# Two layers of windowed attention and MLP on one core: the bias of the second MLP matrix kept in SBUF, and another order for the row maxima of a layer's first unit

## The chip, the cores and the metric

The kernel runs on one core of one Trainium2 chip. The time is device microseconds from a timed run of the whole program; three runs of the kernel before gave 1558.01, 1560.52 and 1563.2 us, so the median is 1560.52 us. The engines are named as the profile names them: PE is TensorE's matmul, PEld its weight load, DVE is VectorE, ACT is ScalarE, POOL is GpSimd, SP is SyncE, which here issues most DMAs.

## The reference

The input is one sequence of 2048 rows by 640 columns. Two layers run one after the other with the same weights; each is an attention block and an MLP block with a residual:

```python
x = A_x
for _ in range(2):
    x = x + A(layernorm(x), wqkv, wo)
    x = x + B(layernorm(x), w1, b1, w2, b2)
# A: 32 heads of 20; query i sees keys i-255..i; softmax; @ wo
# B: h = y @ w1 + b1;  h = max(h, 0)**2;  out = h @ w2 + b2
```

## The kernel before

**Units.** The rows are cut into 8 groups of 256. A group in a layer is a unit, so there are 16 units, u = 0 to 15; u = 0 and u = 8 are the first units of the layers. A unit's attention is worked in 8 quads of 4 heads each. Dense products are done three times over in two-byte floats (high times high, high times low, low times high), so TensorE has many short matmuls (`mm3`, L339).

**One unit's stages.** `stage_qk` and `stage_v` make q, k and v. For each quad, `max_quad` computes the scores once to take each row's maximum ("m" step), `exp_quad` computes them again with the maximum folded in and takes the exponential ("s" step, L825, with masks on POOL L854 and DVE L863), and `pv_quad` multiplies with v ("v" step, L931). `load_o` and `stage_o` divide and apply wo (L1056 adds to the residual), a layer norm follows (L365 to L378), `stage_y` or `y_cross` transposes y, and `stage_f` does the MLP: for each two of the 12 chunks of h, ACT takes the relu with b1 (L1120), POOL squares (L1124), ACT casts the high part (L1127), DVE subtracts for the low part (L1130). Then the second matrix follows and DVE adds to the residual (L1159).

**The bias of the second matrix.** Each `stage_f` first calls `add_b2`: SP loads b2, spread over 128 partitions, into one of the two rotating "xt" buffers (L1069), and POOL adds it to the residual in four pieces (L1076). The xt buffers also hold the rows that a layer norm loads (L430) and the y of `stage_o`. `ln_cross`, which loads the rows of a later unit, is put behind these additions in the plan.

**The row maxima.** A unit that is not the first of its layer has four quarters of keys per window (`quarters(u)` is true). Its scores lie in two PSUM tiles of three banks, `bb6[0]` and `bb6[1]`; each tile's maxima are one merge (L717) and one reduction (L720), and those of the second tile are put into the list `behind`. The function `tops()` issues what lies there; `pv_quad` calls it after its products are issued, and those products use a free half bank of `bb6[1]`. A layer's first unit has no earlier rows; its branch takes eight maxima per quad, each with the mask added (L683), alternating between the tiles (e = 0, 1) for each of four windows.

**What sets the order.** All instructions of all engines are put in order by hand. A planner in the kernel (`Job`, `post`, `pump`) keeps a clock for each engine with booked durations, issues jobs whose start lies within 250 ns of TensorE's planned time, and takes lower `prio` numbers first; a DMA books its size over a rate as traffic. `together` walks through the steps of a unit's quads, makes the maxima of quads that lie `LEAD` = 3 ahead within the v steps, and fills with dense work whenever a step isn't ready. Each engine runs its own queue in order. The maxima of unit 0 are made by `flow`, before the loop over the units; those of unit 8's quads 0 to 2 are made in unit 7's v steps, and its other five in its own.

The flag `later` is passed in `together` alone:

```python
max_quad(m, kind == "v" and quarters(what[1] // NQ))
```

**The start.** During the first units the weights are still loaded and split into high and low parts (`convert`, L271 on ACT, L272 on DVE); the second matrix comes in 12 loads issued by ACT (L324), and b1 is loaded by SP (L1369), behind the work of `load_o(0)`.

Of the kernel before, what the change touches and what calls it, by code (L numbers as in the profile page):

```python
# [10 lines left out]
F32 = mybir.dt.float32  # L11
# [3 lines left out]
ALU = mybir.AluOpType  # L15

P = 128
Q = P // 2
S = 2048
D = 640  # L20
# [4 lines left out]
T = 256  # L25
# [20 lines left out]
def kernel(ctx: ExitStack, tc: tile.TileContext, x, wqkv, wo, w1, b1, w2, b2, out):  # L46
    nc = tc.nc
# [3 lines left out]
    sb = ctx.enter_context(tc.tile_pool(name="sb", bufs=1))  # L51
# [14 lines left out]
    maskw = sb.tile([P, 2 * P], BF16, name="maskw")  # L66
# [15 lines left out]
    for h in range(2):  # L82
        nc.gpsimd.tensor_copy(drop[h * Q:(h + 1) * Q], edges[h * Q:(h + 1) * Q, :, h * Q:(h + 1) * Q])
    b1s = sb.tile([P, FC], F32, name="b1s")
    kts = []
    for i in range(3):
        kts.append(sb.tile([P, NP, T], F16, name=f"kt{i}"))
# [56 lines left out]
    def post(eng, cost, fn, *deps, wait=0.0, prio=1, **kw):  # L144

        j = Job(eng, cost, fn, [d for d in deps if d is not None], now[0] + wait, prio, **kw)
        k = len(pend)
        while k and pend[k - 1].prio > prio:
            k -= 1
        pend.insert(k, j)  # L150
        return j
# [5 lines left out]
    def dma(fn, size, *deps, n=1, cost=450.0, prio=1, **kw):  # L157

        return post("S", n * cost, fn, *deps, prio=prio, size=size, **kw)
# [18 lines left out]
    def need(*js):  # L178

        for j in js:  # L180
            while j.end is None:
                pass_time()
            now[0] = max(now[0], j.end)
# [453 lines left out]
    bbjobs = []  # L637
    bb6 = [ps.tile([P, 3, 512], F32, name=f"bb{e}") for e in range(2)]

    def banks():  # L640
        need(*bbjobs)
        bbjobs.clear()
        return bb6

    def quarters(u):

        return u % NG != 0

    def by_tiles(pieces):

        at, order = {}, []
        for k, (tile, cols, put) in enumerate(pieces):
            order.append((at.get(tile, 0), k, put))
            at[tile] = at.get(tile, 0) + cols
        for _, _, put in sorted(order, key=lambda o: o[:2]):
            for e in range(2):
                put(e)

    behind = []

    def tops():

        for f in behind:
            f()
        behind.clear()

    def max_quad(n, later=False):

        u, qd = divmod(n, NQ)
        g = u % NG  # L670
        qt, cur, prev = qts[u], kts[u % 3], kts[(u - 1) % 3]
        G = qd // GQ
        if (u, G) not in mxs:
            mxs[u, G] = sb.tile([P, 2, 2 * GQ, 2], F32, name="mx", bufs=2)
        mx = mxs[u, G]
        need(trips[u, 0, qd], trips[u, 1, qd])
        bb = banks()

        accum = {(e, w): mx[:, e, (2 * qd + w // 2) % (2 * GQ), w % 2:w % 2 + 1] for e in range(2) for w in range(4)}

        def reduce(e, w, v, mask, cols):
            bbjobs.append(post("D", 113 + 1.047 * cols, lambda:
                               nc.vector.tensor_tensor_reduce(out=v, in0=v, in1=mask, scale=1.0, scalar=-3.0e38,  # L683
                                                              op0=ALU.add, op1=ALU.max, accum_out=accum[e, w]),
                               prio=urgency["turn"]))

        if quarters(u):
            flat = [b.rearrange("p a n -> p (a n)") for b in bb]
            pieces = []
            for w in range(4):  # L690
                j, i = divmod(w, 2)
                p, at = 2 * qd + j, 5 * Q * w
                cuts = sorted({0, 5 * Q, *(z - at for z in (512, 1024) if 0 < z - at < 5 * Q)})
                for o0, o1 in zip(cuts, cuts[1:]):
                    for h in range(2):
                        for kt, lo, hi, to in ((prev, 0, T - i * P, i * P), (cur, T - i * P, 3 * P, i * P - T)):
                            a, b = max(lo, o0 + h * Q), min(hi, o1 + h * Q)
                            if a >= b:
                                continue

                            def put(e, kt=kt, a=a, b=b, to=to, h=h, p=p, i=i, o=at + a - h * Q):
                                r, rows = slice(64 * e, 64 * e + 3 * DH), slice(64 * h, 64 * (h + 1))
                                nc.tensor.matmul(flat[e][rows, o:o + b - a], qt[r, p, i * P + 64 * h:i * P + 64 * (h + 1)],  # L703
                                                 kt[r, p, a + to:b + to], start=True, stop=True,
                                                 tile_position=(64 * e, 64 * h))

                            pieces.append((h, b - a, put))
            by_tiles(pieces)
            now[0] += 690.0
            apart[0] = True  # L710
            for e in range(2):
                wins = flat[e][:, :4 * 5 * Q].rearrange("p (w c) -> p w c", c=5 * Q)
                later = maskq.bitcast(mybir.dt.uint16).unsqueeze(1).to_broadcast([P, 4, Q])
                most = mx[:, e, 2 * qd % (2 * GQ):2 * qd % (2 * GQ) + 2, :].rearrange("p n i -> p (n i)")

                def merge(wins=wins, later=later):
                    nc.vector.copy_predicated(wins[:, :, 4 * Q:], later, wins[:, :, :Q])  # L717

                def top(wins=wins, most=most):
                    nc.vector.tensor_reduce(most, wins[:, :, Q:], axis=mybir.AxisListType.X, op=ALU.max)  # L720

                def both(merge=merge, top=top):
                    j = post("D", 330, merge, prio=urgency["turn"])
                    bbjobs.append(post("D", 1130, top, j, prio=urgency["turn"]))
                    mxjobs[u, G] = list(bbjobs)

                behind.append(both)
                if not (later and e):
                    tops()
        else:  # L730
            for w in range(4):
                j, i = divmod(w, 2)
                for e in range(2):
                    r, p = slice(64 * e, 64 * e + 3 * DH), 2 * qd + j
                    nc.tensor.matmul(bb[e][:, w % 3, w // 3 * T:w // 3 * T + (1 + i) * P], qt[r, p, i * P:(i + 1) * P],
                                     cur[r, p, :(1 + i) * P], start=True, stop=True)
            now[0] += 530.0
            apart[0] = True
            for w in range(4):
                j, i = divmod(w, 2)  # L740
                for e in range(2):
                    to = bb[e][:, w % 3, w // 3 * T:w // 3 * T + (1 + i) * P]
                    if i:
                        reduce(e, w, to, maskw, 2 * P)
                    else:
                        reduce(e, w, to, maskw[:, P:], P)
            mxjobs[u, G] = list(bbjobs)

    mxjobs = {}

# [215 lines left out]
    ols = {}  # L966
# [98 lines left out]

    def add_b2(u):

        b2s = sb.tile([P, D], F32, name="xt", tag="xt", bufs=2)
        load = dma(lambda: nc.sync.dma_start(b2s, bass.AP(tensor=b2.tensor, offset=b2.offset, ap=[[0, P], [1, D]])),  # L1069
                   P * D * 4)  # L1070
        js = []
        for i in range(2):
            for h in range(2):
                hs = slice(h * HD, (h + 1) * HD)
                js.append(post("G", 827, lambda x1=x1s[u, i], hs=hs:
                               nc.gpsimd.tensor_tensor(x1[:, hs], x1[:, hs], b2s[:, hs], op=ALU.add), load, prio=2))  # L1076
        return js

    def y_cross(u):
# [22 lines left out]
    def stage_f(u, ahead=None):  # L1102
# [3 lines left out]
        need(*js)  # L1106
        y2 = y2s.pop(u)
        b2j = add_b2(u)
        hh = sb.tile([P, 2, FC, T], F16, name="hh", tag="hh", bufs=1)
        hj = []  # L1110
# [119 lines left out]
    def together(ns, ms, dense, cost, share=1.0, whole=True, after=None, pace=0):  # L1230
# [26 lines left out]
        for k, (part_, what, m) in enumerate(ts):  # L1257
# [17 lines left out]
            if m is not None:  # L1275
                max_quad(m, kind == "v" and quarters(what[1] // NQ))
# [90 lines left out]
    flow(todo, rest)  # L1367
    load_o(0)
    dma(lambda: nc.sync.dma_start(b1s, b1.rearrange("(c p) -> p c", p=P)), 8192, *ols[0][2], prio=2)  # L1369

    while not all(j.end is not None and j.end <= now[0] + LOOK for j in bbjobs):
        c = next(rest)
# [56 lines left out]
```

## Time and profile before

| What | Value |
|---|---|
| median of 3 runs | 1560.52 us (1558.01 to 1563.2) |
| profiled execution: its time, its span | 1561.46 us, 1559.6 us |
| mean granted TensorE clock | 0.997 |
| busy: PE, PEld, DVE, ACT, POOL | 98%, 77%, 67%, 43%, 29% |
| DMA moved | 162.16 MB, mean 104 GB/s |
| SP's DMA queue | 38.7% of 16 engines |

A share of busy time is an average over the whole span. The granted clock is 1 where TensorE runs at 2.4 GHz and 0.5 at 1.2 GHz. In rows of a timeline a bracket says how long the engine was idle before the instruction and what ended this.

### The profile page before, as it was taken

The page shows a single profiled execution, that of the slowest core. Times are in us where ns is not written, and L with a number is a line of the kernel's source. Part 1 is how long each engine was busy: PE and PEld are TensorE (multiplying, and loading weights), DVE is VectorE, ACT ScalarE, POOL GpSimd, SP SyncE. Part 2 cuts the span into 40 slices and gives each one's busy share as a digit, 9 for nine tenths or more (in the row PEclk, how much of TensorE's full clock was granted, in tenths as well). Part 3 has the DMA queues.
Part 4 walks back from the last instruction along what each step waited for, and adds up shares of the span by engine and source line. Part 5 has one row for each costly group of instructions (what it writes and reads, how often), then busy time and mean ns, then how long its engine had stood idle before and what let it go on. Part 6 is the DMA issues. An engine that isn't in the chain of part 4 may idle for free. (4 is left out here: it accounts for less than half of the span.)

```text
span 1559.6 us, 58897 instructions
## 1 busy us (share of the span) xinstructions
PE 1533.5 (98%) x25822; PEld 1198.6 (77%) x25822; DVE 1043.3 (67%) x2244; ACT 669.7 (43%) x1365; POOL 451.8 (29%) x847
## 2 busy tenths in 40 slices
PE   8998999999999999999999999999999999999999
PEld 6666778787787877878777787877878777786777
DVE  8878775666757667675666757667675676667642
ACT  4565435334453443435343453444435335354422
POOL 1223314232141331413224141321413214142412
PEclk9999999999999999999999999999999999999999
DMA  9975354352534424344462434425243342542120
GB/s 271 209 201 127 80 121 92 106 114 54 123 88 114 105 74 126 69 126 89 99 130 63 119 91 119 100 70 132 67 126 89 94 117 65 122 90 59 30 68 18
DMA packets 248745, 162.16 MB, mean 104 GB/s; under 512 B 96552, under 2 KB 232232, under 8 KB 248488
## 3 DMA queue, kind: packets, MB, share of 16 engines
q1 hardware_dynamic: 242120, 148.89, 38.7%
q10 hardware_dynamic: 6368, 9.50, 2.1%
q8 instruction: 202, 3.31, 0.9%
q14 instruction: 55, 0.45, 0.1%
HBM read 84.68 MB, written 52.95 MB: 88 GB/s over the span
## 5 line engine op out<-in xcount | busy, mean ns | idle before, releaser
L825 ACT ACTIVATE pt<-bb 128x640 f32<-128x640 f32 (+2 forms) x512 | 311.9, 684 | 167.6 <-PE bb L840 148.9
L854 POOL TENSOR_SCALAR_AFFINE_SELECT pt<-pt 64x256 f32<-64x256 f32 x448 | 199.3, 445 | 582.1 <-ACT pt L825 560.0
L339 PE MATMUL acc<-y,w_s 128*128 128x256 f16 x2880 | 330.2, 274 | 1.2 <-DVE y L390 1.2
L339 PE MATMUL acc<-w_s,hh 128*128 128x320 f16 (+1 forms) x2340 | 326.7, 297 | 0.1
L339 PEld LDWEIGHTS <-w_s 128*128 128x128 f16 x2880 | 276.4, 98 | 40.9 <-issue 2.0
L339 PEld LDWEIGHTS <-hh 128*128 128x128 f16 x2340 | 222.1, 98 | 86.8 <-issue 0.4
L720 DVE TENSOR_REDUCE mx<-bb 128x4 f32<-128x1024 f32 x224 | 273.2, 1224 | 6.8
L339 PE MATMUL acc<-yT,wq_s 128*128 128x256 f16 x2250 | 259.1, 273 | 3.0 <-DVE qd L537 1.2
L339 PEld LDWEIGHTS <-wq_s 128*128 128x128 f16 x2400 | 229.6, 98 | 37.3 <-issue 4.3
L863 DVE COPY_PREDICATED_SCALAR pt<-drop,zero 128x256 f32 x224 | 99.9, 497 | 134.3 <-ACT pt L825 133.8
L1130 DVE TENSOR_TENSOR hh<-r,hh 128x256 f16<-128x256 f32 x192 | 98.3, 525 | 110.8 <-ACT hh L1127 105.7
L931 PE MATMUL pv<-pt,vt 64*32 64x192 f32 (+5 forms) x3840 | 166.7, 302 | 0.9 <-DVE y L390 0.6
L943 ACT COPY ot<-pv 128x256 f32<-128x256 f32 x128 | 47.6, 372 | 276.1 <-PE bb L931 247.2
L1124 POOL TENSOR_TENSOR r<-r 128x256 f32<-128x256 f32 x192 | 121.9, 655 | 127.9 <-ACT r L1120 125.3
L931 PE MATMUL bb<-pt,vt 64*32 64x128 f32 (+3 forms) x3584 | 153.5, 301 | 0.0
L717 DVE COPY_PREDICATED bb<-maskq,bb 128x256 f32<-128x256 uint16 x224 | 93.8, 423 | 85.7 <-PE bb L703 80.0
L931 PEld LDWEIGHTS pv<-pt,vt 64*32 64x32 f32 (+1 forms) x3840 | 125.5, 106 | 31.7 <-issue 3.7
L339 PE MATMUL acc<-wo_s,od 128*128 128x320 f16 x960 | 139.6, 299 | 2.2 <-ACT od L1024 2.0
L339 PE MATMUL acc<-wq_s,yT 128*128 128x320 f16 x900 | 132.1, 302 | 5.0 <-DVE qd L537 4.2
L1120 ACT ACTIVATE r<-acc,b1s 128x256 f32<-128x256 f32 x192 | 81.1, 476 | 98.6 <-PE acc L339 96.5
L339 PEld LDWEIGHTS <-od 128*128 128x128 f16 x960 | 90.9, 98 | 40.6 <-ACT od L1024 2.3
L339 PEld LDWEIGHTS <-yT 128*128 128x128 f16 x900 | 87.1, 98 | 40.0 <-issue 6.2
(103 smaller groups left out, 1476.3 us busy)
## 6 DMA issues: line engine op xcount, KB each, us to landing
qt<-qk SPq DMA_DIRECT2D x30, 480.0 KB
kt<-qk SPq DMA_DIRECT2D x30, 480.0 KB
o<-ot SPq DMA_DIRECT2D x256, 42.0 KB
qk<-qd SPq DMA_DIRECT2D x15, 640.0 KB
od<-o SPq DMA_DIRECT2D x14, 640.0 KB
qk<-yl SPq DMA_DIRECT2D x13, 640.0 KB
xt<-in_A_x_dram SPq DMA_DIRECT2D x16, 320.0 KB
x<-in_A_x_dram SPq DMA_DIRECT2D x16, 320.0 KB
```

Source lines behind the costliest of these rows:

```text
L339: nc.tensor.matmul(acc, lhs(a, c), rhs(b, c), start=(k == 0), stop=(k == 3 * nk - 1))
L717: nc.vector.copy_predicated(wins[:, :, 4 * Q:], later, wins[:, :, :Q])
L720: nc.vector.tensor_reduce(most, wins[:, :, Q:], axis=mybir.AxisListType.X, op=ALU.max)
L825: return lambda: nc.scalar.activation(room_of(box)[:, a:b], bank[:, a:b], AF.Exp, scale=SCALE / (QS * QS))
L854: nc.gpsimd.affine_select(out=m, in_=m, pattern=[[0, 4], [-1 if k else 1, Q]], base=0, fill=0.0, compare_op=ALU.is_gt if k else ALU.is_ge, ...
L863: nc.vector.copy_predicated(m, drop[:, k:k + 1, :].bitcast(mybir.dt.uint16).to_broadcast([P, 4, Q]), zero.unsqueeze(1).to_broadcast([P, 4, ...
L931: nc.tensor.matmul(pv[h][32 * jj:32 * (jj + 1), q0 * Q:(q0 + w) * Q], vf[r, c:c + 32], boxes[e]["pt"][r, a:b], start=(k == 0), stop=(k == ...
L943: nc.scalar.copy(ot[:, qd % 2], to)
L1120: nc.scalar.activation(box["r"], acc[:, f, :], AF.Relu, bias=b1s[:, f0 + f:f0 + f + 1], scale=1.0 / (YS * WS))
L1124: nc.gpsimd.tensor_tensor(box["r"], box["r"], box["r"], op=ALU.mult)
L1130: nc.vector.tensor_sub(hh[:, 1, f, :], box["r"], hh[:, 0, f, :])
```

## The change

b2 gets a tile of its own, loaded once, behind b1's load; `add_b2` uses it in all 16 units. In the branch for a layer's first unit the maxima are issued tile by tile; those of the second tile go through `behind`, and `tops()` is called at once where `later` isn't set.

```diff
+    b2s = sb.tile([P, D], F32, name="b2s")
...
-            for w in range(4):
-                j, i = divmod(w, 2)
-                for e in range(2):
-                    to = bb[e][:, w % 3, w // 3 * T:w // 3 * T + (1 + i) * P]
-                    if i:
-                        reduce(e, w, to, maskw, 2 * P)
-                    else:
-                        reduce(e, w, to, maskw[:, P:], P)
-            mxjobs[u, G] = list(bbjobs)
+            def each(e):
+                for w in range(4):
+                    i = w % 2
+                    reduce(e, w, bb[e][:, w % 3, w // 3 * T:w // 3 * T + (1 + i) * P], maskw[:, (1 - i) * P:], (1 + i) * P)
+                mxjobs[u, G] = list(bbjobs)
+
+            each(0)
+            behind.append(lambda: each(1))
+            if not later:
+                tops()
...
     def add_b2(u):
-        b2s = sb.tile([P, D], F32, name="xt", tag="xt", bufs=2)
-        load = dma(lambda: nc.sync.dma_start(b2s, bass.AP(tensor=b2.tensor, offset=b2.offset, ap=[[0, P], [1, D]])),
-                   P * D * 4)
         js = []
         for i in range(2):
             for h in range(2):
                 hs = slice(h * HD, (h + 1) * HD)
                 js.append(post("G", 827, lambda x1=x1s[u, i], hs=hs:
-                               nc.gpsimd.tensor_tensor(x1[:, hs], x1[:, hs], b2s[:, hs], op=ALU.add), load, prio=2))
+                               nc.gpsimd.tensor_tensor(x1[:, hs], x1[:, hs], b2s[:, hs], op=ALU.add), *b2load, prio=2))
         return js
...
     dma(lambda: nc.sync.dma_start(b1s, b1.rearrange("(c p) -> p c", p=P)), 8192, *ols[0][2], prio=2)
+    b2load = [dma(lambda: nc.sync.dma_start(b2s, bass.AP(tensor=b2.tensor, offset=b2.offset, ap=[[0, P], [1, D]])),
+                  P * D * 4, *ols[0][2], prio=2)]
```

## Rows read from the trace of the kernel before

**Rows 1.** Engine shares of the page: busy us, share of the span, instructions.

```profile
PE 1533.5 (98%) x25822; PEld 1198.6 (77%) x25822; DVE 1043.3 (67%) x2244; ACT 669.7 (43%) x1365; POOL 451.8 (29%) x847
```

**Rows 2.** Busy time by stretches: length, busy of each engine, PEclk, DMA share, GB/s.

```profile
0.00:160.00 160.00, 145.16 (x1837) 109.77 (x1838) 128.84 (x344) 83.36 (x164) 40.75 (x82) 0.97 0.75 198
160.00:725.00 565.00, 562.93 (x10215) 443.22 (x10213) 383.46 (x755) 239.19 (x482) 161.92 (x305) 1.00 0.42 101
...
830.00:1320.00 490.00, 489.38 (x8696) 384.70 (x8694) 329.51 (x647) 208.59 (x426) 145.15 (x271) 1.00 0.39 98
1320.00:1510.00 190.00, 184.76 (x3359) 141.69 (x3358) 124.79 (x248) 80.59 (x163) 55.15 (x105) 1.00 0.29 74
```

**Rows 3.** Waits of PE from 160 to 1320: us in total, times, longest.

```profile
PE bb L840 <- issue: 2.3, 3, 1.1
```

**Rows 4.** DMA issues of the bias: count, KB of each.

```profile
xt<-in_B_b_dram SPq DMA_DIRECT2D x16, 320.0 KB
```

**Rows 5.** Timeline of SP near 719: start, us, instruction.

```profile
719.45 0.44 SPq L1069 DMA_DIRECT2D xt<-in_B_b_dram  x1
```

**Rows 6.** Timeline of POOL: start, us, instruction, count, idle before and its releaser.

```profile
723.03 0.86 POOL L1076 TENSOR_TENSOR x<-x,xt 128x320 f32<-128x320 f32 x1 [6.62 <-DMA xt<-in_B_b_dram]
...
247.39 0.86 POOL L1076 TENSOR_TENSOR x<-x,xt 128x320 f32<-128x320 f32 x1 [8.83 <-DMA xt<-in_B_b_dram]
...
253.59 2.09 POOL L1076 TENSOR_TENSOR x<-x,xt 128x320 f32<-128x320 f32 x2
```

**Rows 7.** Timeline of DVE, the low parts of h near 253 and 258.

```profile
253.53 1.43 DVE L1130 TENSOR_TENSOR hh<-r,hh 128x256 f16<-128x256 f32 x2 [1.92 <-ACT hh L1127]
...
258.69 0.75 DVE L1130 TENSOR_TENSOR hh<-r,hh 128x256 f16<-128x256 f32 x2
```

**Rows 8.** Timeline of PE near 258.

```profile
258.54 0.75 PE L840 MATMUL bb<-qt,kt 62*64 62x128 f16 x37 [0.33 <-DVE ot L946]
```

**Rows 9.** Timeline of SP from 129 to 145.

```profile
131.24 0.40 SPq L1369 DMA_DIRECT2D b1s<-in_B_b_dram  x1
136.49 0.36 SPq L1069 DMA_DIRECT2D xt<-in_B_b_dram  x1
```

**Rows 10.** Timeline of ACT from 122 to 142, loads and conversions of w2.

```profile
122.97 0.33 ACTq L324 DMA_DIRECT2D kt<-in_B_w_dram  x1
...
128.22 0.74 ACT L271 ACTIVATE w_s<-kt 128x640 f16<-128x640 f32 x1 [1.77 <-DMA kt<-in_B_w_dram]
...
131.81 0.34 ACTq L324 DMA_DIRECT2D kt<-in_B_w_dram  x1
...
138.81 1.36 ACT L271 ACTIVATE w_s<-kt 128x640 f16<-128x640 f32 x2
141.15 0.80 ACT L389 CAST y<-tr 128x384 f16<-128x384 f32 x2 [0.98 <-PE tr L403]
```

**Rows 11.** Busy time by stretches, as rows 2, around 139.

```profile
128.00:139.60 11.60, 8.37 (x178) 5.92 (x176) 11.05 (x25) 5.76 (x11) 3.04 (x6) 1.00 0.53 149
139.60:146.40 6.80, 5.80 (x58) 4.28 (x59) 5.77 (x11) 4.50 (x8) 1.51 (x1) 0.53 0.02 5
```

**Rows 12.** Timeline of DVE, maxima of unit 8's first quad.

```profile
743.95 0.30 DVE L683 CUSTOM_DVE_ANT_0 bb<-bb,maskw 128x128 f32<-128x128 f32 x1 [1.03 <-PE bb L931]
...
746.20 0.14 DVE L683 DVE_READ_ACCUMULATOR2_ANT mx<- 128x1 f32 x1
```

**Rows 13.** Waits of DVE from 725 to 830: us in total, times, longest.

```profile
DVE bb L683 <- PE bb L931: 2.0, 2, 1.0
```

**Rows 14.** Timeline of PE near 140.

```profile
140.24 1.30 PE L403 MATMUL tr<-ident,xt 128*128 128x128 f32 x5 [1.78 <-DVE xt L378]
```

**Rows 15.** Timeline of DVE near 139.

```profile
138.34 1.22 DVE L720 TENSOR_REDUCE mx<-bb 128x4 f32<-128x1024 f32 x1
139.49 0.60 DVE L378 TENSOR_SCALAR xt<-x,bmv 128x640 f32<-128x640 f32 x1
```

**Rows 16.** Timeline of PE near 1441.

```profile
1441.23 0.45 PE L339 MATMUL acc<-wo_s,od 128*128 128x320 f16 x2 [1.97 <-ACT od L1024]
```

## The prediction

> **What bounds the kernel now.** I read the engine shares first: TensorE is busy for 1533.5 of 1559.6 us, 98%, and no other engine passes 67% [rows 1]. An average can hide stages, so the busy time by stretches comes next [rows 2]. From 160 to 725 us TensorE is busy for 562.93 of 565.00 us, from 830 to 1320 us for 489.38 of 490.00. What is not busy lies at the two ends: 160.00 - 145.16 = 14.8 us in the first 160 us and 190.00 - 184.76 = 5.2 us from 1320 to 1510. Then TensorE's own waits from 160 to 1320 us: the largest group is 2.3 us "issue" [rows 3], and the next, 0.3 us, is one wait that comes up below. Over 1160 us, some 13 of the 16 units, nothing that another engine or a DMA does late reaches TensorE, apart from these. An edit can shorten the time only by taking TensorE work away (this one takes none) or at the ends; it can lengthen it by making something late that is now covered.
>
> **The first edit, the bias.** Before, each of the 16 calls of the second dense stage loads 320 KB [rows 4] into one of the two "xt" buffers, and four GpSimd additions wait for it. After, one load lands in a tile of its own, and 15 go: 15 x 0.328 = 4.9 of 162 MB. In steady units the load issues at 719.45 and the first addition starts at 723.03, 3.6 us later [rows 5, 6]. GpSimd stands still before it, 6.62 us there and 8.83 us in another unit at 247.39 [rows 6], because the addition is first in its queue. But what queues behind it (the squares L1124 and the masks L854) is made well ahead of TensorE: none of TensorE's waits in the middle is for GpSimd. So:
> - Taken off SyncE: 15 issues of 0.44 us [rows 5]. What stands behind them on that queue starts sooner by as much; nothing on TensorE waits for it. 0 us.
> - The additions: the same 64 (four a unit), the same 0.86 us [rows 6]. They start when the stage opens, in the gap in which GpSimd now waits. Four take 3.5 us, the gaps are 6.62 and 8.83 us. They then no longer lie between the squares, where they slow VectorE: at 253.53 two L1130 take 1.43 us beside the two additions of 253.59, at 258.69 a pair without them 0.75 us [rows 6, 7]. I let 1.43 - 0.75 = 0.68 us come off the chain L1130, L717, L720, L717, L720, L946 there, at whose end TensorE waits 0.33 us at 258.54 [rows 8]. That wait goes: -0.3 us. It is the only TensorE wait in the middle that I can tie to the bias. Bounds: 0 if the squares alone keep L1130 slow, -0.33 if not; nearest row says -0.3.
> - The Trainium skill, "SBUF — State Buffer", section "Who interferes with whom", says that a VectorE instruction with two SBUF inputs and a GpSimd instruction that reads SBUF shut each other out for a whole instruction. The 1.43 us agree. By that rule the squares shut L1130 out as well, so moving the additions alone might give 0 here instead of -0.3 us.
> - The buffers: "xt" rotates over four allocations per unit where it was five. The next layer norm's loads take the slots of the two y tiles, read long before. No wait appears; none of TensorE's waits in the middle is on that path. 0 us.
> - The single load is put behind b1's, which SyncE issues at 131.24, so it goes out at about 131.7 where the first bias load now goes at 136.49 [rows 9]. Nothing on SyncE stands between. It is 5 us earlier, in a stretch where three loads of the second MLP matrix start (the first at 131.81) [rows 10]. The DMA engines are 0.53 busy at 149 GB/s there [rows 11], so full rate by these rows is about 281 GB/s (an estimate) and 0.328 MB cost 1.17 us. A load issued at 122.97 was awaited until 128.22, 5.25 us later; one issued at 131.81, held up by 1.17 us, lands at 138.2, and its conversion on ScalarE starts at 138.81 now [rows 10]. Cover of 0.6 us there, and of 0.98 us more before TensorE is touched, since ScalarE's next step on the way to it, L389 at 141.15, has that much idle time in front of it [rows 10]. So 0; the price when it fails is the slower rival below. The planner, which books 1.0 us of traffic (size over rate) at this point, may shift those conversions by as much.
>
> **The second edit, the row maxima.** The branch for a layer's first unit issues its eight maxima tile by tile instead of alternating, in both layers; total work is the same. "Behind the products" needs the flag that is set only when the maxima of this unit are made inside the v turns of a unit with four quarters: with a lead of three quads these are the second layer's first three quads, 24 of the 128 maxima. For the other 13 quads only the order changes: 0 us. At the first of the three, the second maximum, which is on the second tile, waits 1.03 us until the products with v end, and the six behind it are held [rows 12]. VectorE has two such waits from 725 to 830 us, 2.0 us in all [rows 13]. With the first tile's four in front they are filled. So VectorE gains 2.0 us at most, where TensorE does not wait for it: its waits over this stretch are among those of the middle [rows 3]. On the path: 0 us. Bounds: below, nothing, since no wait is there to shorten; above, the four late maxima could hold the next quad's scores in each of three quads: seven take 746.34 - 743.95 = 2.39 us [rows 12], four so 1.4, three times that 4.1 us. I take 0, the value of the waits that are in the rows now, and because the planner puts dense matmuls ahead of whatever waits.
>
> **The sum.** -0.3 + 0 + 0 = -0.3 us. The profiled execution took 1561.46 us (span 1559.6), 0.94 above the median of 1560.52. So 1561.2 against the profiled execution, 1560.2 against the median.
>
> **Rivals.**
> - *Faster: the start falls into another order.* The order of instructions is worked out by a greedy planner, so each edit may shuffle what follows it. From 128 to 139.6 us TensorE is idle for 11.60 - 8.37 = 3.2 us, from there to 146.4 for 1.0 us [rows 11], 4.2 us together; the longest wait, 1.78 us [rows 14], is for VectorE's L378, which starts at 139.49 because a reduction of 1.22 us, L720, stands ahead of it [rows 15]. After these waits the granted clock is 0.53 from 139.6 to 146.4 [rows 11], so most of it is at 1.2 GHz, where 5.80 us are busy: 5.80 x 0.47 = 2.7 us lost. All of it gone: -6.9 us, 1553.6; more likely the 1.78 us and the clock, -4.5 us, 1556. For it: the edit moves a DMA right there. Against it: nothing in the edit moves L717/L720 or L378 on purpose.
> - The Trainium skill, "TensorE: Matmul & The Clock Gate", section "HAM oscillation — how this bites in real kernels", says that waits of the engine bring its clock down and the work behind starts slow. Here the row after 139.6 agrees, but a wait of 1.97 us at 1441 is followed by no slow row (clock 1.00 for 1320 to 1510) [rows 2, 16]. By the rule alone every such gap would be worth more than its length; by the rows only the cluster at the start is.
> - *Slower: the one bias load collides with the second matrix's loads.* If it delays them by more than 0.6 us, ScalarE, which takes its queue in order, stands at the conversion of 138.81; from 0.6 + 0.98 = 1.6 us on, the transposed second half of y behind it (L389), which TensorE needs next, is late, and there it decides. One delay of 1.17 us is under that; if each of the three loads loses as much, the last comes 3.5 us late: 3.5 - 1.6 = 1.9 us of TensorE wait, and another stretch at 1.2 GHz like the one seen, 2.7 us: +4.6 us, 1565.1. For it: 0.75 of the DMA share is in use over the first 160 us [rows 2]. Against it: at that very point 0.53 [rows 11].
> - *The maxima held behind the products make the next scores late*: +4.1 us, 1564.6. Against it: the whole stretch has no such wait to begin with.
> - *The flag does nothing* (three quads only, no wait on TensorE): this is inside the forecast; the time would be the same.
>
> **How the numbers follow.** Forecast, no change that can be told: 0.69. Other order at the start: 0.18, of which about 0.14 pass 4.7 us. Load collision 0.08, late maxima 0.05. A difference under 0.3% (4.7 us) is what a measurement of this kernel can hardly tell from none: the three runs alone lie from 1558.01 to 1563.2. Small reorderings at the two ends, which hold 14.8 + 5.2 us of waits, carry 0.05 of the forecast out on either side. So faster is 0.14 + 0.05 = 0.19; slower 0.05 and, since both slower rivals end close to the bound, about half of their 0.13, together 0.12; same the rest, 0.69. The range reaches 1.7 us past the partial faster rival and to the two slower ones: 1554.3 to 1565.0.
>
> **What would show it.** Right: TensorE busy for the same 1533 us; no GpSimd wait at the additions; the additions ahead of the first squares in each unit; the TensorE wait near 258 us gone; VectorE's two waits of 1.0 us near 744 and 767 us gone with the next scores where they were. Wrong: TensorE waits in the middle that name the maxima or the masks; the ScalarE conversions of the second matrix waiting for DMA near 138 us; a change of the waits or of the half-clock row between 128 and 147 us by over 4 us.

## The result and the profile after

The changed kernel takes 1567.82 us (1565.04 to 1569.71, six runs) beside 1560.65 for the kernel before (1558.01 to 1563.2, six runs): ratio 1.0044, 95% interval 1.003 to 1.0058. It is slower, by some 4.7 to 9 us, and above the range of the prediction. The profiled execution took 1567.73 us. In the profile after, lines stand one or two numbers off: L684 is the maximum that was L683, L888 the score products that were L886, L704 the matmul that was L703.

The engine shares first [rows 1]:

```profile
PE 1534.5 (98%) x25822; PEld 1198.3 (77%) x25822; DVE 1047.6 (67%) x2244; ACT 669.7 (43%) x1365; POOL 449.3 (29%) x847
```

TensorE does the same 25822 matmuls in 1 us more of busy time, but the span is 5.3 us longer (1564.9 against 1559.6). VectorE is busy 4.3 us longer with the same 2244 instructions. The busy time by stretches (length; busy us of PE, PEld, DVE, ACT and POOL; granted clock; DMA share; GB/s), each cut 5 us later than in [rows 2] because the work has slid by 5 us:

```profile
0.00:165.00 165.00, 146.32 (x1835) 109.60 (x1836) 134.09 (x344) 82.96 (x164) 41.36 (x81) 0.96 0.72 192
165.00:730.00 565.00, 563.71 (x10225) 444.00 (x10224) 382.14 (x756) 240.25 (x485) 163.70 (x309) 1.00 0.41 98
730.00:835.00 105.00, 103.49 (x1299) 79.67 (x1297) 66.51 (x223) 45.53 (x103) 33.82 (x66) 1.00 0.38 89
835.00:1325.00 490.00, 489.47 (x8693) 384.68 (x8694) 327.62 (x648) 208.59 (x425) 144.39 (x271) 1.00 0.39 95
1325.00:1515.00 190.00, 184.98 (x3383) 141.92 (x3368) 124.81 (x248) 80.83 (x163) 54.86 (x105) 1.00 0.28 71
```

The middle is as full as before, but for the stretch of unit 8 from 730 us on, where TensorE idles 1.51 us; the same stretch of the kernel before has 0.30:

```profile
725.00:830.00 105.00, 104.70 (x1312) 80.77 (x1311) 63.75 (x223) 46.42 (x105) 37.20 (x70) 1.00 0.43 96
```

The first stretch takes 165 us for what took 160: 1835 matmuls against 1837. So most of the loss is at the start. A narrower window finds it. Both rows hold 613 matmuls, the same but for one at each end, in the kernel before and then after:

```profile
33.00:95.50 62.50, 60.70 (x613) 42.81 (x613) 46.15 (x176) 30.78 (x66) 11.89 (x28) 0.97 0.87 208
```

```profile
33.00:100.10 67.10, 62.39 (x613) 43.62 (x613) 50.78 (x175) 30.54 (x65) 12.71 (x28) 0.95 0.81 194
```

They take 67.10 us in place of 62.50: 4.60 us, most of the 5.3 us. TensorE idles 4.71 us of it instead of 1.80 (2.91 more), and the matmuls are busy 1.69 us longer at a lower mean clock. These are the quads of unit 0. TensorE's waits from 33 to 101 us, after:

```profile
PE acc L340 <- DVE qd L538: 4.2, 1, 4.2
PE bb L888 <- DVE mx L684: 1.6, 2, 0.9
PE tr L791 <- DVE mx L684: 1.0, 1, 1.0
```

The 4.2 us are in the trace of before as well, and lie for the most part ahead of the window, before the matmul that opens it. New are the two groups for the maxima of L684, 2.6 us; before, no wait in this window names them. (One wait of 0.5 us for GpSimd is new too.) Now VectorE. The first quad of unit 0, the first of its eight maxima and the readout of the last, in the kernel before:

```profile
34.23 0.30 DVE L683 CUSTOM_DVE_ANT_0 bb<-bb,maskw 128x128 f32<-128x128 f32 x1 [0.90 <-PE bb L735]
34.45 0.14 DVE L683 DVE_READ_ACCUMULATOR2_ANT mx<- 128x1 f32 x1
34.45 0.33 DVE L683 CUSTOM_DVE_ANT_0 bb<-bb,maskw 128x128 f32<-128x128 f32 x1
34.70 0.14 DVE L683 DVE_READ_ACCUMULATOR2_ANT mx<- 128x1 f32 x1
34.70 0.47 DVE L683 CUSTOM_DVE_ANT_0 bb<-bb,maskw 128x256 f32<-128x256 f32 x1
35.08 0.14 DVE L683 DVE_READ_ACCUMULATOR2_ANT mx<- 128x1 f32 x1
35.08 0.47 DVE L683 CUSTOM_DVE_ANT_0 bb<-bb,maskw 128x256 f32<-128x256 f32 x1
...
36.72 0.14 DVE L683 DVE_READ_ACCUMULATOR2_ANT mx<- 128x1 f32 x1
```

and after:

```profile
34.91 0.30 DVE L684 CUSTOM_DVE_ANT_0 bb<-bb,maskw 128x128 f32<-128x128 f32 x1 [1.74 <-PE bb L736]
35.13 0.14 DVE L684 DVE_READ_ACCUMULATOR2_ANT mx<- 128x1 f32 x1
35.31 0.43 DVE L684 CUSTOM_DVE_ANT_0 bb<-bb,maskw 128x256 f32<-128x256 f32 x1
35.66 0.14 DVE L684 DVE_READ_ACCUMULATOR2_ANT mx<- 128x1 f32 x1
35.83 0.30 DVE L684 CUSTOM_DVE_ANT_0 bb<-bb,maskw 128x128 f32<-128x128 f32 x1
...
36.57 0.14 DVE L684 DVE_READ_ACCUMULATOR2_ANT mx<- 128x1 f32 x1
36.57 0.33 DVE L684 CUSTOM_DVE_ANT_0 bb<-bb,maskw 128x128 f32<-128x128 f32 x1
...
38.27 0.14 DVE L684 DVE_READ_ACCUMULATOR2_ANT mx<- 128x1 f32 x1
```

Before, a maximum begins in the same instant as the readout of the one in front of it (34.45 and 34.45, 34.70 and 34.70). After, it begins when that readout is over (35.13 + 0.14, then 35.31). The one exception is 36.57, where the second tile follows the first. A maximum writes the masked scores in place, and in the program's instructions each carries a wait for VectorE's last write to its tile. In alternating order that write lies two maxima back and is done in time. Tile by tile it is the maximum directly in front, in six of eight cases. The four windows of a tile lie in separate pieces of it (`w % 3`, `w // 3 * T` in the change), so the results do not need this wait; it goes by the tile. The eight take 36.86 - 34.23 = 2.63 us before and 38.41 - 34.91 = 3.50 us after: 0.87 us more, 0.145 us for each of the six.

The Trainium skill, "VectorE: DVE Perf Modes", section "The DRAIN you can't avoid", says that VectorE empties its pipeline after every instruction, and that with eight copies in a row a semaphore after each cost nothing extra. For these maxima the rows show otherwise, and the measurement decides: without a wait the next one overlaps the readout, with one it does not.

In that stretch TensorE has too little other work to cover this. Its timeline of after, where it waits and behind it:

```profile
42.59 0.27 PE L791 MATMUL tr<-ident,mx 128*16 128x128 f32 x1 [0.95 <-DVE mx L684]
...
88.83 0.49 PE L888 MATMUL bb<-qt,kt 62*128 62x256 f16 x7 [0.91 <-DVE mx L684]
...
90.11 0.70 PE L340 MATMUL acc<-yT,wq_s 128*128 128x256 f16 x5 [0.58 <-DVE stg L538]
90.77 1.55 PE L704 MATMUL bb<-kt,qt 60*64 60x256 f16 x38
```

The 38 matmuls at 90.77 take 1.55 us; the same 38 in the trace of before take

```profile
87.56 1.03 PE L703 MATMUL bb<-kt,qt 60*64 60x256 f16 x38
```

The granted clock tells why, in a stretch of after:

```profile
90.00:93.40 3.40, 3.29 (x59) 2.09 (x58) 1.44 (x5) 1.61 (x4) 1.53 (x4) 0.62 0.65 199
```

A mean of 0.62 is mostly 1.2 GHz. TensorE had waited 0.91 and 0.58 us just ahead of it. Of the 3.29 us busy there some 1.25 (0.38 of them, an estimate) are lost to the clock: most of the 1.69 us of longer busy time.

The bias part moved as forecast. GpSimd's additions [rows 6] now run in one go and ahead of the squares, with no wait for a load; SyncE's load [rows 9] stands behind b1's; and the two matmul groups at [rows 8] have no wait between them. GpSimd, SyncE and TensorE of after:

```profile
243.83 3.33 POOL L1075 TENSOR_TENSOR x<-x,b2s 128x320 f32<-128x320 f32 x4
```

```profile
135.67 0.40 SPq L1368 DMA_DIRECT2D b1s<-in_B_b_dram  x1
136.11 0.96 SPq L1369 DMA_DIRECT2D b2s<-in_B_b_dram  x1
```

```profile
260.83 2.35 PE L340 MATMUL acc<-y,w_s 128*128 128x256 f16 x20
263.10 0.76 PE L842 MATMUL bb<-qt,kt 62*64 62x128 f16 x38
```

### The profile page after: what moved, and what is told of

The parts are those of the page before. It is cut to its first block, busy times and chain, and to the rows that moved or that the text cites. A ratio compares the mean times of both kernels' runs of the same rounds, so it can differ in the third digit from the quotient of the medians.

```text
span 1564.9 us, 58817 instructions
## 1 busy us (share of the span) xinstructions
PE 1534.5 (98%) x25822; PEld 1198.3 (77%) x25822; DVE 1047.6 (67%) x2244; ACT 669.7 (43%) x1365; POOL 449.3 (29%) x847
## 5 line engine op out<-in xcount | busy, mean ns | idle before, releaser
L1129 DVE TENSOR_TENSOR hh<-r,hh 128x256 f16<-128x256 f32 x192 | 91.7, 491 | 106.8 <-ACT hh L1126 101.7
L933 PE MATMUL bb<-pt,vt 64*32 64x64 f32 (+3 forms) x3584 | 153.6, 301 | 0.0
```

The source lines that it names most:

```text
L933: nc.tensor.matmul(pv[h][32 * jj:32 * (jj + 1), q0 * Q:(q0 + w) * Q], vf[r, c:c + 32], boxes[e]["pt"][r, a:b], start=(k == 0), stop=(k == ...
L1129: nc.vector.tensor_sub(hh[:, 1, f, :], box["r"], hh[:, 0, f, :])
```

## Experiments

Times are medians; a ratio, with its 95% interval, is against the kernel before, timed beside it on the same chip.

**The two halves of the change.** The bias edit alone:

> The bias edit alone; the row maxima alternate between the tiles as before. Theory A (the loss is made by the order of the maxima: with the tiles no longer alternating, each maximum has to wait for the one before it on its own tile, about 0.12 us a time, 0.87 us a quad, and in unit 0 TensorE has no cover for it): no change, 1558 to 1562 us, TensorE idle in the first 160 us as before (14.8 us). Theory B (the single bias load, 5 us earlier, or the additions, now in another place on GpSimd, make the loss): 1565 to 1569 us, with ScalarE or GpSimd late before 160 us.

1560.09 against 1560.84 us, ratio 0.9999 (0.999 to 1.0007). The row order alone:

> The order of the maxima alone; the bias is loaded 16 times as before. Theory A: all of the loss, 1565 to 1569 us, eight maxima of a quad take 3.5 us where they took 2.6. Theory B: 1558 to 1562 us.

1566.12 against 1560.84, ratio 1.004 (1.0025 to 1.0055). The loss is the order of the maxima; the bias is worth nothing that can be told.

**Which of the quads.** Tile by tile in unit 0 alone, the rest of the change as it is:

```diff
-            def each(e):
+            if u == 0:
+                def each(e):
...
+            else:
+                ...
```

> The whole change, but tile by tile only in unit 0; in unit 8 the maxima alternate as before. Theory A: nearly all of the loss stays, 1564 to 1568 us, since only in unit 0 does TensorE wait for the maxima (waits of 0.7 to 1.0 us at 42, 73 and 88 us). If the loss came from unit 8 (the second tile's maxima behind the products, waits near 763 and 786 us): 1559 to 1562 us.

1564.64, ratio 1.0026 (1.0017 to 1.0034). Then the same with `if u > 0:`, so in unit 8 alone:

> The whole change, but tile by tile only in unit 8; in unit 0 the maxima alternate as before. Theory A: 1559 to 1562.5 us, the small TensorE waits of 0.35, 0.97 and 0.31 us between 760 and 880 us remain and cost 1 to 1.6 us; the half-clock stretch near 90 us is gone. If the loss came from unit 8: 1564 to 1568 us.

1561.98, ratio 1.0005 (0.9996 to 1.0013). And with `if later:`, in the three quads whose maxima really stand behind the products with v:

> The whole change, but tile by tile only in the three quads of unit 8 whose second tile's maxima stand behind the products; the other 13 quads alternate as before. Theory A: no loss, 1558.5 to 1562 us; VectorE's two waits of 1.0 us near 744 and 767 us are gone, but each of the three quads takes 0.9 us longer on VectorE, so that nothing is gained.

1561.22 against 1560.58, ratio 1.0005 (0.9996 to 1.0014). Unit 0 carries most of the loss. Unit 8 shows no change of time that can be told by itself. In the last of these kernels the wait of VectorE that the edit was to fill is filled: unit 8's first quad runs so, and no second wait stands in it ([rows 12] had one of 1.03):

```profile
740.44 0.30 DVE L684 CUSTOM_DVE_ANT_0 bb<-bb,maskw 128x128 f32<-128x128 f32 x1 [0.34 <-PE bb L736]
...
743.79 0.14 DVE L684 DVE_READ_ACCUMULATOR2_ANT mx<- 128x1 f32 x1
```

VectorE gains little by it: the quad takes 743.93 - 740.44 = 3.49 us where it took 3.78 with its wait, because six new waits for the tile stand in it.

**Is it the wait for the tile, or the order itself?** The row order alone, with the masked scores written to two scratch tiles in turn instead of in place (both orders give the same maxima, and nothing reads the masked scores afterwards):

```diff
+    junk = [sb.tile([P, 2 * P], F32, name=f"junk{i}") for i in range(2)]
...
-    nc.vector.tensor_tensor_reduce(out=v, in0=v, ...
+    nc.vector.tensor_tensor_reduce(out=junk[w % 2][:, :cols], in0=v, ...
```

> The order of the maxima alone, tile by tile, but each masked score goes to one of two scratch tiles in SBUF in turn instead of back onto the scores, so that no maximum writes what the next one reads. Theory A (the wait for the maximum before it on the same tile is the loss): eight maxima of a quad take 2.6 to 2.8 us again, the TensorE waits of 0.7 to 1.0 us for maxima before 100 us are gone, 1559 to 1562.5 us. Rival C (tile by tile is slow in itself, because two reductions in a row read the same tile of PSUM): 3.5 us a quad still, 1564 to 1569 us.

1559.57 against 1560.58, ratio 0.9995 (0.9986 to 1.0004): the loss is gone with the order unchanged. VectorE there:

```profile
34.45 0.29 DVE L684 CUSTOM_DVE_ANT_0 junk<-bb,maskw 128x128 f32<-128x128 f32 x1 [1.22 <-PE bb L736]
34.67 0.08 DVE L684 DVE_READ_ACCUMULATOR2_ANT mx<- 128x1 f32 x1
34.67 0.42 DVE L684 CUSTOM_DVE_ANT_0 junk<-bb,maskw 128x256 f32<-128x256 f32 x1
35.01 0.08 DVE L684 DVE_READ_ACCUMULATOR2_ANT mx<- 128x1 f32 x1
...
36.68 0.09 DVE L684 DVE_READ_ACCUMULATOR2_ANT mx<- 128x1 f32 x1
```

Each begins with the readout in front of it again. But the readout is also shorter (0.08 against 0.14), and eight take 36.77 - 34.45 = 2.32 us, less than before. So a write to SBUF could be the cure by itself. One scratch tile in place of two tells that apart (`junk[0]` for `junk[w % 2]`):

> The run before with two scratch tiles (maxima tile by tile, 1559.57 us, eight maxima of a quad in 2.3 us), with one scratch tile in place of two: every maximum now writes the tile that the one before it wrote, from SBUF as before. Theory A (an instruction of VectorE that follows one that wrote the same tile starts only when that one is through, some 0.13 to 0.17 us later): the waits are back, seven in a quad instead of six, so a quad's eight take 2.3 + 7 x 0.145 = 3.3 us (3.1 to 3.6), and the time is again 1563 to 1567 us. Rival D (the two scratch tiles helped because a write to SBUF is quicker than a write in place to PSUM, and the waits were never the price): the eight take 2.3 to 2.5 us as with two tiles, and the time is 1558 to 1561.

1563.39 against 1560.59, ratio 1.002 (1.001 to 1.0029): slower again.

```profile
34.92 0.29 DVE L684 CUSTOM_DVE_ANT_0 junk<-bb,maskw 128x128 f32<-128x128 f32 x1 [1.74 <-PE bb L736]
35.14 0.08 DVE L684 DVE_READ_ACCUMULATOR2_ANT mx<- 128x1 f32 x1
35.26 0.42 DVE L684 CUSTOM_DVE_ANT_0 junk<-bb,maskw 128x256 f32<-128x256 f32 x1
35.61 0.08 DVE L684 DVE_READ_ACCUMULATOR2_ANT mx<- 128x1 f32 x1
...
38.12 0.08 DVE L684 DVE_READ_ACCUMULATOR2_ANT mx<- 128x1 f32 x1
```

The waits are back, the eight take 38.20 - 34.92 = 3.28 us, and TensorE waits for the maxima again, from 33 to 101 us:

```profile
PE bb L888 <- DVE mx L684: 1.2, 2, 0.7
PE tr L791 <- DVE mx L684: 0.8, 1, 0.8
```

Between these two kernels the instructions, their order and the memories of their operands are the same; only the tile written by the neighbour differs, and the time differs by 3.8 us. That is the cause, shown. The old order with two scratch tiles (one for each score tile) completes the square:

> The kernel before, alternating order and 16 bias loads as they are, with the masked scores written to two scratch tiles, one for each of the two score tiles. Theory A: no wait either, so the eight maxima of a quad take 2.3 us as with tile by tile and two scratch tiles; TensorE hardly waits for maxima before, so the time stays at 1559 to 1561.5, and against the scratch kernel in tile by tile order (1559.57) it tells what the order is worth once it costs no wait: the two waits of 1.0 us for the products with v near 744 and 767 us are back and change nothing (within 1 us). Rival (the order tile by tile is itself a gain that the waits hid): over 2 us slower than the scratch kernel in tile by tile order.

1559.76 against 1560.59, ratio 0.9991 (0.9982 to 1.0001); eight take 36.57 - 34.27 = 2.30 us. Once it costs no wait, the order is worth nothing: the two waits of [rows 13], 2.2 us in this trace, are back and the time is the same as with the scratch kernel above.

**A smaller dose.** The kernel before, with four same-tile neighbours in a quad instead of none or six:

```diff
+            for e, w in ((0, 0), (0, 1), (1, 0), (1, 1), (0, 2), (0, 3), (1, 2), (1, 3)):
```

> The kernel before, with the maxima in pairs: two of the first tile, two of the second, and so on, all ahead of the products. Four of eight maxima follow one on their own tile, where the change has six and the kernel before none. Theory A, by dose: 4 x 0.145 us = 0.6 us a quad more, eight take 3.2 us, two thirds of the loss, 1562 to 1565 us. If the loss came from the second tile's maxima being late as a block (first tile's four all in front): none of it, 1559 to 1562 us.

1562.2 against 1560.58, ratio 1.0011 (1.0003 to 1.002). The eight take 37.35 - 34.15 = 3.20 us: 0.57 us more than before, 0.143 for each of the four. The price of a wait holds. The time rises by 1.6 us, under a third of the 5.3 of the row order alone and not the two thirds expected. TensorE's waits for the maxima, from 33 to 101 us, grow with the duration of the eight: none at 2.63 us a quad, 1.2 us at 3.20, 2.0 at 3.28 (one scratch tile), 2.6 at 3.50 (row order alone). That looks as if other work still covered a first part of the delay. The times rise by 1.6, 2.8 and 5.3 us.

**The whole once more:**

> The whole change once more, timed in as many rounds as its parts. If the parts add up (bias -0.75 against its kernel before, unit 0's maxima +3.8 with the bias in, unit 8's +1.1 with the bias in, so about 3.8 + 1.1 + 0.75 = 5.7 us), it comes out at 1565 to 1567.5 us. If the bias and the maxima make each other worse, it stays at the 1567.8 seen at first or above.

1566.49 against 1560.59, ratio 1.0031 (1.002 to 1.0042), 5.9 us by the medians. The parts give 3.8 for unit 0 and 1.1 for unit 8, each with the bias edit in, so that its -0.75 is counted once too often: 3.8 + 1.1 + 0.75 = 5.7. They add up, within what can be measured. No kernel here beats the one before by more than its interval. The scratch tiles and the resident bias were not run together.

## Why the prediction was wrong

**The step that failed** is in the second edit: "total work is the same" and "For the other 13 quads only the order changes: 0 us". The order does set the work's duration. A quad's eight maxima went from 2.63 to 3.50 us. In unit 0 seven quads grew by this and the fourth, which waits for ScalarE in its midst, from 4.32 to 4.46: some 6.2 us more in all on VectorE. TensorE had lost 4.6 us by 100 us: 2.91 of idle and 1.69 of slower matmuls. The readings were at hand. The rows of [rows 12] show seven maxima in 2.39 us, 0.34 each, though one of them is busy 0.30 or 0.47 us and its readout 0.14: they overlap, and the prediction never asked what lets them.

**The cover was read in the wrong stretch.** "Nothing that another engine or a DMA does late reaches TensorE" rests on [rows 2, 3], from 160 us on. Unit 0's quads lie between 33 and 100 us, inside the first 160 us, where the prediction itself counted 14.8 us of idle TensorE. It looked at 128 to 147 us of these only, for the load and for another order.

**The bias, -0.3 us: nothing that can be told, and its sign is not shown.** The additions lie ahead of the squares, and four take 3.33 us (3.5 forecast). Alone the edit measures -0.75 us by the medians and -0.2 by the ratio, whose interval (-1.6 to 1.1 us) holds -0.3 and 0. The wait near 258 is gone in all six traces with this edit. But of the five other kernels with the old loads only one still has it (two scratch tiles in the new order, 0.41 us), so its going can't be put down to the edit.

**The load collision: not there; the additions collide instead.** TensorE's wait for VectorE's L379 [rows 14] has grown by 0.59 us:

```profile
145.24 1.13 PE L404 MATMUL tr<-ident,xt 128*128 128x128 f32 x5 [2.37 <-DVE xt L379]
```

The load did not make it. ScalarE's conversion, which was to wait, waits for no DMA there. L379 itself takes 1.19 us, beside two of GpSimd's additions, where it took 0.60 [rows 15]. ScalarE, GpSimd and VectorE of after:

```profile
143.22 1.36 ACT L272 ACTIVATE w_s<-kt 128x640 f16<-128x640 f32 x2
```

```profile
143.07 1.67 POOL L1075 TENSOR_TENSOR x<-x,b2s 128x320 f32<-128x320 f32 x2
```

```profile
143.91 1.19 DVE L379 TENSOR_SCALAR xt<-x,bmv 128x640 f32<-128x640 f32 x1
```

All six traces with the bias edit show 1.19 us here and the wait of 2.37; all six with the old loads show 0.60 and 1.78. So the additions were moved off one VectorE instruction and onto another one that TensorE waits for. The prediction priced the first, -0.3 us, and put their new place at nothing. In the time of the bias edit alone this can't be told, so the rival's time is out as well. The half-clock stretch behind the wait was there before too [rows 11].

**The three late quads: right.** VectorE's waits for the products with v are gone, and TensorE gains nothing by it. The rival that they make the next scores late (+4.1 us) gets no support: by themselves they measure +0.6 us, within the interval. That rival had the right place (TensorE waiting for maxima) but the wrong mechanism and the wrong unit, and its time, 1564.6, is close to the 1564.64 of unit 0 alone only by chance.

**Another order at the start: out.** The queues of TensorE and ScalarE hold the same instructions in the same order in both kernels, and VectorE's differ in the maxima alone. The planner books a maximum at a fixed time whatever stands in front of it, so it saw nothing to rearrange.

Open: in the trace of after the clock falls at 90 us, and in the repeat of the whole the 38 matmuls take 1.55 us there again; with unit 0 alone they take 1.03, though the waits ahead are alike (1.6 and 1.0 us in all). That trace has its slow stretch earlier:

```profile
32.00:40.00 8.00, 7.10 (x39) 3.61 (x39) 4.46 (x19) 0.65 (x2) 0.00 (x0) 0.57 0.89 205
88.00:95.00 7.00, 5.50 (x89) 3.72 (x88) 5.47 (x17) 3.42 (x8) 1.53 (x4) 1.00 0.59 174
```

From 32 to 40 us the kernel before has a granted clock of 0.79 where this one has 0.57. But the kernel with tile by tile in unit 8 alone, whose unit 0 alternates, has 0.57 there as well. So how much of the 1.69 us belongs to the order, and how much to the execution, is not settled. The wait near 1441 us [rows 16] is a like case: the trace of before shows no slow row behind it, and the trace of the bias edit alone shows a granted clock of 0.79 from 1438 to 1446 us.

What unit 8 adds is seen in the traces and not in the time. By itself its interval holds zero, but TensorE waits there once, which before it did not:

```profile
786.09 1.25 PE L340 MATMUL acc<-wq_s,yT 128*128 128x320 f16 x8 [0.97 <-DVE qd L538]
```

This wait goes with the waits for the tile in unit 8's later quads. It is 1.0 us in the four traces with six in a quad, 0.8 with one scratch tile and 0.7 with pairs; where these quads have no such wait (six traces) it is not there.

## What to carry to other kernels

When instructions of one engine are put into another order, look at which tile each writes and which tile its new neighbour writes: alternating two tiles can be what lets them overlap, and an output that nobody reads is still a tile to wait for. "Only the order changes" is a cost to be measured, here by the distance between starts in a timeline rather than by busy time. And check the cover in the very stretch where the edit lies: a kernel that is 98% busy on TensorE may have none at its start. The same goes for work that is moved on a second engine: ask what it will lie beside.

## What the hardware showed that was not expected

- Two maxima of VectorE in succession overlap by the length of the accumulator readout, 0.14 us, unless the second waits for the first. A wait costs 0.145 us with the scores masked in place in PSUM. With all eight writing the same SBUF tile, seven waits cost 3.28 - 2.32 = 0.96 us, unevenly: six maxima begin 0.11 to 0.12 us behind the start of the readout in front, and the fifth, which needs the second score tile from TensorE as well, 0.23 us.
- The accumulator readout takes 0.14 us behind a maximum that writes PSUM and 0.08 us behind one that writes SBUF, and the maxima are a little shorter too: eight take 2.30 us instead of 2.63 in the same alternating order.
- VectorE's busy time tells little of the loss. Over the 128 maxima it rises from 41.3 to 45.9 us, while the mean of one falls from 392 to 369 ns: maxima that overlap are longer each, and the time that they share is counted once.
- A VectorE instruction of 0.60 us (L379) takes 1.19 us beside two GpSimd additions; six traces with them there and six without agree.
